# The first MoE's weight transfers on GpSimd's queue instead of SyncE's, in an attention + two-MoE kernel

## The chip, the cores and the metric

The kernel runs on one core of a Trainium2 chip. The metric is the device time of one execution in microseconds, lower being better. Before the change it is 1120.15 us, the median of three runs from 1114.83 to 1122.45.

## The reference

Three stages follow each other. All inputs are float32 in the reference; the weights reach the device as 64-bit floats.

```
# attention: batch 4, 12 heads, 448 tokens, head width 64
q_n, k_n = rmsnorm(q, g_q), rmsnorm(k, g_k)
attn = softmax(q_n @ k_n^T / sqrt(64));  attn_out = attn @ v
x = attn_out as [1792 tokens, 768]
# first MoE (one expert, no routing): 768 -> 1024 -> 768
h = x @ w_in;  solu = h * softmax(h);  ln = layernorm(solu) * g_ln;  x = ln @ w_out
# second MoE: 768 -> 2048 -> 768
h = x @ w_in;  g = h - tanh(h);  out = g @ w_out
```

## The kernel before

Products that need more than TensorE's reduced float32 are made of three matmuls: every operand is split into a high and a low part (`split`, the two halves of `w`), and `three` (L181 to L184) adds high x high, high x low and low x high. So a weight tile has two halves, each as large as the float32 weights.

**Weights.** `Stream` (L96 to L178) hands out a list of weight tiles in the order of their use. A tile is a 256 x 512 or 512 x 256 piece of a matrix in the form that the device gets (pairs of 32-bit words), 512 KB. `fetch` loads it raw (L115) into one of two buffers `raw`; `convert` turns the 64-bit values into float32 on ScalarE and VectorE, makes the high part on ScalarE and the low part on GpSimd (L161, for the input matrices) or VectorE (L155, for `w_out` of the first MoE). The result, again 512 KB, lies in one of five buffers `w`. With `save` it is stored to device memory (L164), and where the list names a tile a second time (`again`), L174 reloads that stored form instead. The first MoE's stream is `ws`: 12 tiles of `w_in` and 12 of `w_out` are loaded raw, converted and stored, `w_in` is reloaded for three of the four token blocks and `w_out` for all four. The second MoE's stream, `w2`, loads and converts 48 tiles and stores none.

**Order of the work.** Attention goes by pairs of heads, 24 in all. Its steps stand in a list sorted by slots, two slots a pair: keys and queries are loaded, normalised (`norm`, its last step `qn` at L258 on GpSimd), transposed and split (`qk_trans`), and copied by SyncE's transfers to other partitions (L301, L305 for queries, L307, L308 for keys). `maxima` gives the row maxima, `spread` puts them into the query tile by a small transfer (L355), `weights` makes the exponentials, `pv` the product with the values, `x_norm` divides and stores the result to `xd` (L432). `load_v` clears a value tile on GpSimd (L222) and loads it (L224, L228).

The first MoE goes over four token blocks `b` (384, 384, 384 and 640 tokens). `stage(b)` reads a block of attention's output (`x_split`, L496), makes the block's input product (`moe_h`, matmuls into `hps`, four quarters of 256 columns, three weight tiles each), its layer norm (one power on GpSimd at L563 for each 128 tokens), and the output product of the block before (`moe_x2`, into `x2ps`). `moe_h` asks for the next quarter's three tiles after the first tokens of the current one, by

```
if t0 == blocks[b][0][0] and tp == 0:
    ws.conv(w0 + 3 * qq + 6)
```

`overlap` writes the steps of a batch's attention between those of a stage in proportion to estimated costs. The second MoE follows, apart from its first six tiles and its first inputs, which are converted ahead of the first MoE's last stages.

The engines don't run in the written order exactly: the launch makes `TileContext(nc, schedule_with_timeline_sim=True)`, whose scheduler simulates times and lets each engine take the next instruction that is ready by its account. The order on each engine is then fixed, and each engine runs it strictly in turn. Waits on buffers are put in by the same layer. All transfers are issued by SyncE but three tiny ones of constants, which ScalarE issues.

Of the kernel before, what the change touches and what calls it, by code (L numbers as in the profile page):

```python
# [8 lines left out]
F32 = mybir.dt.float32  # L9
# [9 lines left out]
def kernel(  # L19
# [14 lines left out]
    nc = tc.nc  # L34
# [47 lines left out]
    def source(kind, i):  # L82
        if kind == "out":
            d, half = divmod(i, 2)
            src = moe_w_out[512 * half:512 * half + 512, 256 * d:256 * d + 256]
            return src.rearrange("(c p) (f z) -> p c f z", p=128, z=2), (4, 128)
        r, c = divmod(i, 3)
        if kind == "out2":
            src = moe2_w_out[256 * r:256 * r + 256, 512 * c:512 * c + 512]
        else:  # L90
            src = (moe_w_in if kind == "in" else moe2_w_in)[256 * c:256 * c + 256, 512 * r:512 * r + 512]
        return src.rearrange("(c p) (f z) -> p c f z", p=128, z=2), (2, 256)

    saved = {}

    class Stream:  # L96


        def __init__(self, items, pool, save):
            self.items, self.pool, self.save = items, pool, save  # L100
            self.raw, self.got = {}, {}
            self.nl = self.nc = 0
# [8 lines left out]
        def fetch(self, kind, i):  # L111
            if (kind, i) not in self.raw:
                src, (a, b) = source(kind, i)
                t = self.raw[kind, i] = raw_p.tile([128, a, b, 2], I32, tag="raw", name="raw64")
                nc.sync.dma_start(out=t, in_=src)  # L115

        def convert(self, kind, i, pool, save):
            self.fetch(kind, i)
            t = self.raw.pop((kind, i))
            a, b = t.shape[1:3]  # L120
            if kind == "out2":

                if i % 3 == 0:
                    self.wide = pool.tile([128, 2, a, 3 * b], F32R, tag="w18", name="w18")
                w = self.wide[:, :, :, b * (i % 3):b * (i % 3) + b]
            else:
                w = pool.tile([128, 2, a, b], F32R, tag="w6", name="w6")
            val = raw_p.tile([128, a, b], I32, tag="val", name="val")
            hi32 = t[:, :, :, 1].rearrange("p c f -> p (c f)")
            lo32 = t[:, :, :, 0].rearrange("p c f -> p (c f)")  # L130
            vv = val.rearrange("p c f -> p (c f)")

            fv, fh = vv.bitcast(F32), hi32.bitcast(F32)
            if save:
                nc.scalar.activation(out=fv, in_=fh, func=AF.Abs)
                nc.vector.tensor_scalar(out=fv, in0=fv, scalar1=2.0 ** -15, scalar2=None, op0=ALU.max)
            else:
                nc.gpsimd.tensor_scalar(out=fv, in0=fh, scalar1=2.0 ** -15, scalar2=None, op0=ALU.max)
                nc.vector.scalar_tensor_tensor(out=fv, in0=fh, scalar=-1.0, in1=fv, op0=ALU.mult, op1=ALU.max)
            nc.vector.tensor_scalar(  # L140
                out=vv, in0=vv, scalar1=3, scalar2=0x3FFFFFFF,
                op0=ALU.logical_shift_left, op1=ALU.bitwise_and,
            )
            nc.vector.scalar_tensor_tensor(
                out=vv, in0=hi32, scalar=-0x40000000, in1=vv, op0=ALU.bitwise_and, op1=ALU.bitwise_or
            )
            nc.vector.scalar_tensor_tensor(
                out=vv, in0=lo32, scalar=29, in1=vv, op0=ALU.logical_shift_right, op1=ALU.bitwise_or
            )
            x = val.bitcast(F32)  # L150
            if kind == "out":
                for c in range(4):
                    g = gln[:, 4 * (i % 2) + c:4 * (i % 2) + c + 1]
                    nc.scalar.activation(out=w[:, 0, c], in_=x[:, c], func=AF.Copy, scale=g)
                    nc.vector.scalar_tensor_tensor(  # L155
                        out=w[:, 1, c], in0=x[:, c], scalar=g, in1=w[:, 0, c].bitcast(F32),
                        op0=ALU.mult, op1=ALU.subtract,
                    )
            else:
                nc.scalar.activation(out=w[:, 0], in_=x, func=AF.Copy)  # L160
                nc.gpsimd.tensor_tensor(out=w[:, 1], in0=x, in1=w[:, 0].bitcast(F32), op=ALU.subtract)  # L161
            if save:
                saved[kind, i] = dram.tile([128, 2, a, b], F32, name=f"w_{kind}_{i}")
                nc.sync.dma_start(out=saved[kind, i], in_=w.bitcast(F32))  # L164
            return w

        def conv(self, n):
            while self.nc < min(n, len(self.items)):
                self.load(self.nc + 1)
                kind, i, again = self.items[self.nc]  # L170
                if again:
                    a, b = source(kind, i)[1]
                    w = self.pool(kind, i).tile([128, 2, a, b], F32R, tag="w6", name="w6")
                    nc.sync.dma_start(out=w.bitcast(F32), in_=saved[kind, i])  # L174
                else:
                    w = self.convert(kind, i, self.pool(kind, i), self.save)
                self.got[self.nc] = self.wide if kind == "out2" else w
                self.nc += 1  # L178
                self.load(self.nc + 2)
# [307 lines left out]
    Bp = {}  # L487
# [162 lines left out]
    items, w_at = [], {}  # L650
    for b in range(NBK + 1):
        for d in range(KD + 1):
# [3 lines left out]
            if d < KD and b > 0:  # L656
                w_at["out", b - 1, d] = len(items)
                items += [("out", i, True) for i in (2 * d, 2 * d + 1)]
    ws = Stream(items, lambda kind, i: Bp["w"], True)


    attn_next()
# [61 lines left out]
    items = []  # L724
    for sp in range(NSP):
        items += [("in2", 3 * sp + i, False) for i in range(3)]
        items += [("out2", 3 * sp + i, False) for i in range(3)]
    w2 = Stream(items, next_w, False)
    xs_t, ob = [], {}

    def x2_load(i):
# [109 lines left out]
```

## Time and profile before

| | before |
|---|---|
| median of three runs | 1120.15 us (1114.83 to 1122.45) |
| the profiled execution's own time | 1117.29 us |
| its span in the profile | 1115.4 us |
| TensorE busy (PE) | 1045.5 us, 94% |
| VectorE (DVE), ScalarE (ACT), GpSimd (POOL) busy | 694.8, 493.8, 234.2 us |
| moved by DMA | 171.20 MB, 153 GB/s over the span |
| chain that ended last, by engine | PE 74%, DMA 12%, DVE 7%, ACT 5% |

PE is TensorE's matmuls and PEld its weight loads; DVE is VectorE, ACT ScalarE, POOL GpSimd, SP or SPq SyncE's queue. L12 is line 12 of the kernel. In names such as `w<-w_in` the tile that is written stands in front of what is read; `w_in<-w` is a store of converted weights, `raw<-in_moe_w_in_dram` a raw load, and digits are dropped, so that the second MoE's raw loads bear the same names. A "wait" is idle time of an engine, with what ended it. The chain of waits is followed back from the last instruction, at each step to what released it. The clock column is the granted share of TensorE's full clock.

### The profile page before, as it was taken

To read this page: it belongs to the slowest core of one execution; us is meant where nothing else is said; L and a number is where in the kernel's file an instruction comes from. 1 tells how busy PE (TensorE), PEld (TensorE's weight loads), DVE (VectorE), ACT (ScalarE), POOL (GpSimd) and SP (SyncE) were. 2 spreads that over 40 slices of the span, in tenths; PEclk is the share of its full clock that TensorE was granted. 3 is DMA by queue.
4 is the path that set the end of the run, shared out by engine and by line. 5 is a ranking of instruction groups with operands and counts; after the bars stand their busy time and mean duration, and the time that the engine had idled before them with its cause. 6 is when DMAs were issued, how large, how long until landed. Compare 5 with 4: busy or idle time off the path is not lost.

```text
span 1115.4 us, 15528 instructions
## 1 busy us (share of the span) xinstructions
PE 1045.5 (94%) x5528; PEld 874.9 (78%) x5528; DVE 694.8 (62%) x1313; ACT 493.8 (44%) x1004; POOL 234.2 (21%) x204
## 2 busy tenths in 40 slices
PE   4989999988987899998999999999999999999998
PEld 2555666657774778777899989898999989898987
DVE  8776687788797353724655057375767666675444
ACT  4677777777676454744246154321212121212110
POOL 2411123131102000001500025242314241322000
PEclk9999999999998999998999999999999999999999
DMA  7987779957997978655767443121111111120004
GB/s 184 258 230 192 184 213 282 229 167 209 288 285 231 307 207 260 182 174 174 249 205 242 156 152 92 34 65 49 57 38 57 58 58 57 57 57 1 1 29 170
DMA packets 108945, 171.20 MB, mean 153 GB/s; under 512 B 31748, under 2 KB 73156, under 8 KB 108868
## 3 DMA queue, kind: packets, MB, share of 16 engines
q1 hardware_dynamic: 107568, 170.20, 52.2%
q8 instruction: 44, 0.72, 0.3%
q14 instruction: 33, 0.27, 0.1%
q10 hardware_dynamic: 1300, 0.01, 0.1%
HBM read 109.32 MB, written 29.10 MB: 124 GB/s over the span
## 4 chain that ended last, share of the span: by engine, by line
PE 74%; DMA 12%; DVE 7%; ACT 5%; issue 2%; SPq 1%; POOL 0%; ACTq 0%; DVEq 0%; POOLq 0%
PE pvps L401 8%; PE ops L183 7%; PE ops L184 7%; PE ops L182 7%; PE h2ps L183 7%; PE h2ps L184 7%; PE h2ps L182 7%; PE sps L378 4%; PE x2ps L182 3%; PE x2ps L183 3%; PE x2ps L184 3%; PE hps L182 2%; PE hps L184 2%; DMA xr<-xd 2%; PE hps L183 2%; DMA q<-wq 2%
## 5 line engine op out<-in xcount | busy, mean ns | idle before, releaser
L780 DVE TENSOR_TENSOR ob<-ops,ob 128x384 f32<-128x384 f32 x196 | 108.6, 555 | 103.0 <-PE ops L184 102.4
L161 POOL TENSOR_TENSOR w<-val,w 128x512 fp32r<-128x512 f32 x60 | 81.3, 1356 | 419.7 <-ACT w L160 402.6
L401 PE MATMUL pvps<-pf,va 128*128 128x448 f32 (+1 forms) x384 | 160.9, 583 | 1.7 <-ACT pf L387 1.7
L183 PE MATMUL ops<-w,gT 128*128 128x384 f32 x448 | 150.7, 336 | 0.0
L182 PE MATMUL ops<-w,gT 128*128 128x384 f32 x448 | 150.6, 336 | 0.0
L184 PE MATMUL ops<-w,gT 128*128 128x384 f32 x448 | 150.5, 336 | 0.0
L343 DVE TENSOR_REDUCE nm<-mps 128x1 f32<-128x448 f32 x168 | 102.9, 620 | 66.3 <-PE mps L342 57.6
L183 PE MATMUL h2ps<-x2s,w 128*128 128x512 f32 (+1 forms) x384 | 141.0, 367 | 0.0
L184 PE MATMUL h2ps<-x2s,w 128*128 128x512 f32 (+1 forms) x384 | 140.9, 367 | 0.0
L182 PE MATMUL h2ps<-x2s,w 128*128 128x512 f32 (+1 forms) x384 | 140.6, 367 | 0.0
L378 PE MATMUL sps<-q,k 128*128 128x448 f32 (+1 forms) x368 | 117.5, 413 | 20.7 <-ACT pf L387 9.2
L757 ACT ACTIVATE th<-h2ps 128x512 f32<-128x512 f32 (+1 forms) x64 | 34.8, 544 | 181.2 <-PE h2ps L184 180.9
L378 PEld LDWEIGHTS sps<-q,k 128*128 128x128 f32 (+1 forms) x368 | 63.0, 186 | 55.5 <-ACT pf L387 17.8
L387 ACT ACTIVATE pf<-sps 128x448 f32<-128x448 f32 x167 | 88.3, 539 | 37.9 <-PE sps L378 29.5
L182 PE MATMUL hps<-w,xs 128*128 128x256 f32 x336 | 101.0, 301 | 2.7 <-DMA w<-w_in 2.5
L184 PE MATMUL hps<-w,xs 128*128 128x256 f32 x336 | 96.5, 288 | 0.0
L183 PE MATMUL hps<-w,xs 128*128 128x256 f32 x336 | 95.6, 285 | 0.0
L401 PEld LDWEIGHTS pvps<-pf,va 128*128 128x128 f32 (+1 forms) x384 | 61.6, 195 | 42.1 <-issue 34.3
L342 PE MATMUL mps<-k,q 128*128 128x448 f32 (+1 forms) x144 | 77.2, 545 | 14.9 <-DVE nm L343 5.6
L258 POOL TENSOR_TENSOR qn<-qk,rr 112x512 f32<-112x512 f32 x44 | 47.5, 1101 | 192.5 <-DVE rr L239 88.9
L183 PEld LDWEIGHTS ops<-w,gT 128*128 128x128 f32 x448 | 84.3, 188 | 4.6
L182 PEld LDWEIGHTS ops<-w,gT 128*128 128x128 f32 x448 | 84.2, 188 | 4.6 <-DVE ob L780 0.2
(117 smaller groups left out, 2091.7 us busy)
## 6 DMA issues: line engine op xcount, KB each, us to landing
w<-w_out SPq DMA_DIRECT2D x48, 512.0 KB
raw<-in_moe_w_in_dram SPq DMA_DIRECT2D x36, 512.0 KB
raw<-in_moe_w_out_dram SPq DMA_DIRECT2D x36, 512.0 KB
w<-w_in SPq DMA_DIRECT2D x36, 512.0 KB
k<-wk SPq DMA_DIRECT2D x46, 224.0 KB
q<-wq SPq DMA_DIRECT2D x46, 224.0 KB
w_in<-w SPq DMA_DIRECT2D x12, 512.0 KB
w_out<-w SPq DMA_DIRECT2D x12, 512.0 KB
```

Of the source, the lines that this page charges most:

```text
L161: nc.gpsimd.tensor_tensor(out=w[:, 1], in0=x, in1=w[:, 0].bitcast(F32), op=ALU.subtract)
L182: nc.tensor.matmul(ps, lhsT=a[0], rhs=w[0], start=first, stop=False)
L183: nc.tensor.matmul(ps, lhsT=a[0], rhs=w[1], start=False, stop=False)
L184: nc.tensor.matmul(ps, lhsT=a[1], rhs=w[0], start=False, stop=last)
L258: eng.tensor_tensor(out=qn[:, a].rearrange("p c h d -> p h c d"), in0=t[:, a], in1=rr[:, a].rearrange("p h (c o) -> p h c o", o=1).to_broa ...
L342: nc.tensor.matmul(ps, lhsT=qh[:, f:f + 128], rhs=kh, start=True, stop=True)
L343: nc.vector.tensor_reduce(out=nm_t[p][:, c:c + 1], in_=ps, axis=AX.X, op=ALU.max, negate=True)
L378: nc.tensor.matmul(o, lhsT=K[p % NQ][:, i, z, k0:k0 + m], rhs=qcols(Q[p % NQ], slice(0, 128), p, i, z), start=(z == 0), stop=(z == 1))
L387: nc.scalar.activation(out=x, in_=ps, func=AF.Exp)
L401: nc.tensor.matmul(pv_t[n], lhsT=w, rhs=pc_t.pop((n, j))[r], start=first, stop=last)
L757: nc.scalar.activation(out=th, in_=ps, func=AF.Tanh)
L780: nc.vector.tensor_tensor(out=o, in0=ps, in1=o, op=ALU.add)
```

## The change

The stream gets the issuing engine as an argument. `ws`, the first MoE's stream, gets GpSimd, and `w2`, the second's, SyncE as before. So 24 raw loads, 24 stores and 84 reloads, 132 transfers of 512 KB, are issued by GpSimd.

```
-        def __init__(self, items, pool, save):
+        def __init__(self, items, pool, save, queue):
+            self.queue = queue
...
-                nc.sync.dma_start(out=t, in_=src)
+                self.queue.dma_start(out=t, in_=src)
...
-                nc.sync.dma_start(out=saved[kind, i], in_=w.bitcast(F32))
+                self.queue.dma_start(out=saved[kind, i], in_=w.bitcast(F32))
...
-                    nc.sync.dma_start(out=w.bitcast(F32), in_=saved[kind, i])
+                    self.queue.dma_start(out=w.bitcast(F32), in_=saved[kind, i])
...
-    ws = Stream(items, lambda kind, i: Bp["w"], True)
+    ws = Stream(items, lambda kind, i: Bp["w"], True, nc.gpsimd)
...
-    w2 = Stream(items, next_w, False)
+    w2 = Stream(items, next_w, False, nc.sync)
```

## Rows read from the trace of the kernel before

**Rows 1.** Busy time by stretch: stretch us, engines' busy us (instructions), clock, DMA share, GB/s

```profile
0.00:60.00 60.00, 42.40 (x124) 23.71 (x124) 46.41 (x107) 34.09 (x73) 21.19 (x29) 1.00 0.87 227
...
180.00:240.00 60.00, 54.66 (x278) 38.94 (x279) 46.61 (x96) 43.73 (x92) 12.38 (x12) 0.97 0.89 229
...
300.00:360.00 60.00, 48.46 (x207) 33.19 (x208) 52.66 (x125) 43.56 (x97) 9.12 (x11) 0.91 0.86 260
...
540.00:600.00 60.00, 58.95 (x444) 57.65 (x443) 38.55 (x93) 27.00 (x52) 13.66 (x12) 1.00 0.70 233
600.00:700.00 100.00, 99.51 (x591) 93.47 (x590) 42.78 (x56) 38.69 (x69) 22.48 (x14) 1.00 0.44 141
700.00:1060.00 360.00, 360.00 (x1910) 329.97 (x1909) 228.95 (x391) 77.02 (x136) 98.11 (x66) 1.00 0.15 45
...
0.00:600.00 600.00, 534.97 (x2768) 404.79 (x2768) 399.36 (x826) 371.26 (x789) 113.58 (x124) 0.98 0.79 226
```

**Rows 2.** Waits of TensorE over the span: total us, times, longest us

```profile
PE qkps L268 <- DVE nr L238: 11.0, 1, 11.0
...
PE sps L378 <- DMA q<-nt: 6.3, 4, 2.0
...
PE mps L342 <- DMA q<-wq: 3.4, 2, 1.8
...
PE hps L182 <- DMA w<-w_in: 2.5, 2, 2.0
...
PE x2ps L182 <- DMA w<-w_out: 1.7, 3, 0.6
```

**Rows 3.** The chain of waits in order of time, transfers: start us, us, what

```profile
13.77 6.93 DMA raw<-in_moe_w_in_dram
...
24.21 5.15 DMA q<-wq
...
202.76 8.00 DMA w<-w_in
...
285.76 7.97 DMA q<-wq
...
386.18 9.26 DMA xr<-xd
...
525.93 2.80 DMA xr<-xd
...
542.30 4.79 DMA w<-w_in
```

**Rows 4.** Waits of SyncE's queue, 0 to 600 us: total us, times, longest us

```profile
SPq L115 <- DVE val L147: 32.4, 13, 8.5
SPq L174 <- PE x2ps L184: 30.0, 16, 4.6
SPq L174 <- PE hps L184: 26.9, 16, 9.8
```

**Rows 5.** SyncE's issues by line: duration ns min/median/max, first and last start us

```profile
L174 SPq DMA_DIRECT2D w<-w_out x48: 319/320/1065, 316.3 to 629.6; - x48
L174 SPq DMA_DIRECT2D w<-w_in x36: 320/384/1610, 202.2 to 565.3; - x36
...
L115 SPq DMA_DIRECT2D raw<-in_moe_w_out_dram x17: 373/387/3250, 179.7 to 560.6; - x17
```

**Rows 6.** GpSimd's instructions by line: busy us, mean ns, idle before, releasers

```profile
L258 POOL TENSOR_TENSOR qn<-qk,rr 112x512 f32<-112x512 f32 x44 | 47.5, 1101 | 192.5 <-DVE rr L239 88.9 <-ACT w L154 20.7 <-PE hps L184 19.2
```

**Rows 7.** Timelines of GpSimd, SyncE and TensorE around 542 us: start us, us

```profile
540.07 1.99 POOL L138 TENSOR_SCALAR val<-raw 128x512 f32<-128x512 f32 x1 [1.98 <-DMA raw<-in_moe_w_out_dram]
...
542.30 1.67 SPq L174 DMA_DIRECT2D w<-w_in  x3
...
547.14 0.39 PE L182 MATMUL hps<-w,xs 128*128 128x256 f32 x1 [0.41 <-DMA w<-w_in]
```

## The prediction

> **What bounds the kernel now.** The table by stretch comes first [rows 1]. From 600 us on, in the second MoE, TensorE is busy for 99.51 of 100 us and then 360.00 of 360, and of the moved transfers only the last reloads fall there; nothing is to be won behind that point. Ahead of it lie attention and the first MoE, in which all of the moved transfers run. There TensorE is busy 42.40 of the first 60 us and 54.66, 48.46 and 58.95 in the three other 60-us stretches shown; over the 600 us it is idle for 65 us, of which 17.6 lie in the first 60. The same rows show the DMA engines 0.70 to 0.89 busy: this half is close to DMA-bound as well as close to TensorE-bound.
>
> What TensorE waits for by name is little [rows 2]: 11.0 us once at the start for VectorE, 6.3 + 3.4 us for the small transfers of attention's queries, and 2.5 + 1.7 us for the first MoE's weights. But engines run in order, and a late transfer holds up ScalarE or SyncE before it shows on TensorE. So the chain of waits says more [rows 3]. Between 0 and 600 us, pieces of the chain that are transfers which stay on SyncE's queue (keys and queries, their shifted copies, maxima, attention's output) number 14, the constants' load apart, from the one at 24.21 to the one at 525.93, and sum to 70.6 us. The moved kind (raw weights, stores, reloads) has 8 pieces, from 13.77 to 542.30, sum 48.5 us. A piece is 2.80 us where the queue is quiet and 7.97 or 9.26 us where weights are ahead of it: that difference is what the change can get at.
>
> **What the change does, part by part.** All 132 transfers of 512 KB (24 raw loads, 24 stores, 84 reloads) leave SyncE for GpSimd; sizes, order in the program, buffers and waits stay. Nothing is computed more or less.
>
> *SyncE is relieved.* A moved issue has cost it 0.32 to 0.39 us at the median, and up to 3.25 us when the queue was backed up [rows 5]. By the medians, with the 24 stores put at a raw load's, that is 84 x 0.35 + 48 x 0.39 = 48 us of issuing. It also stood at the head of its queue for 32.4 us until a raw buffer, and 30.0 + 26.9 us until a weight buffer came free [rows 4]; in that time nothing of attention that was queued behind could be issued (a few of the 13 stops on raw buffers are the second MoE's, which stay). None of this is lost one for one, as SyncE is no computing engine: it counts where a staying transfer is late, which is the 70.6 us above. If each of the 14 pieces fell to some 3 us, as the quietest of them, the chain would lose 70.6 - 42 = 28.6 us. That is the far end. The near end is 0: half the bytes in this stage are still the weights', and the engines that move them are the same. I take a third, -9.5 us, because the busy share of the DMA engines stays and because when a transfer comes earlier the next-latest (ScalarE's or VectorE's work, which has the shares of busy time in [rows 1]) takes over.
>
> *The start.* The raw load at 13.77 holds ScalarE's in-order queue for 6.93 us, and the query's copy after it takes another 5.15 [rows 3]. On a queue of its own the raw load can be issued before SyncE is through with the first keys, queries and values. That may take off up to 6.9 us, or cost up to 5.2 when 512 KB loads share the engines with the first heads' inputs. I take -2.
>
> *GpSimd takes 132 issues.* The trace has no transfer issued by GpSimd, so its price is bounded: below by nothing, since GpSimd is busy for only 114 of the 600 us [rows 1] and may do it in idle time; nearest by one of its own ordinary instructions, 1.10 us [rows 6]; above by the longest issue that SyncE had, 3.25 us [rows 5]. I take 1.1 us: 132 x 1.1 = 145 us, spread over 600 us with those 114 in them. It fits. What else is queued on GpSimd behind an issue that waits: the normalised keys and queries (44 of the instructions in [rows 6]) and the clearing of the value tiles. The first stand a whole slot ahead of their transposition in the written order (slot s - 3 against s - 2 and s - 1, two slots a head pair), which covers some microseconds; the clearing waits for TensorE just as the reloads do, in the same order. I put 0 on both; if that cover is gone, a wait of GpSimd for VectorE's norms, 88.9 us in all [rows 6], is what a reload would sit behind. The 14 powers of the layer norm have no such cover: VectorE goes on with their result. One issue in front of every one would be 14 x 1.1 = 15 us of VectorE, off the bound; I put 0 on it, and up to 5 in the range.
>
> *The tight reloads.* In the first MoE's input product, a quarter of the columns needs three weight tiles, five buffers exist, so the third tile of the next quarter is asked for only when TensorE lets go of the first of the current one. By the code that is 3 times in each of 3 blocks: nine reloads. [Rows 7] show one: issued at 542.30, TensorE has 0.41 us of idle time and starts on it at 547.14; the chain has the transfer as 4.79 us [rows 3]. So the lead, about 4.8 us, is spent to the end. An issue of 1.1 us in place of 0.38 adds 0.7 us to each: 9 x 0.7 = +6 us, the value I take; it is 0 if the clear ring gives it back, and the upper end is 9 x (1.1 + 2.0) = 28 us if GpSimd has an instruction of its own as long as the 1.99 us one in [rows 7] in front of each. In the last block that is likely for some, since GpSimd then converts the second MoE's first weights; I add 1.5 us.
>
> The Trainium skill has a price for the same step: "DMA: Bandwidth & Descriptors", section Latency and other measured facts, puts the first byte of a transfer from GpSimd at about 1 us and from SyncE at about 0.6; by it alone the tight reloads would cost 9 x 0.4 = 3.6 us in place of 6 (an estimate from that page), and no row here shows GpSimd's queue.
>
> **Sum.** -9.5 - 2 + 6 + 1.5 = -4 us. The profiled execution took 1117.29 us, of which the span is 1115.4; so 1117.3 - 4 = 1113 us. It lies 3 us under the median of the three runs shown (1120.15), whose own spread is 7.6 us. About 1% is what a measurement of this kernel can tell from no change, and the forecast is 0.6% under the median.
>
> **Rivals.**
> *A, the ring was the brake.* Small transfers no longer stand behind 512 KB ones: the full 28.6 us and the start's 6.9 come off, 1117.3 - 35.5 = 1082 us. For it: pieces of 7.97 and 9.26 us against 2.80 [rows 3]. Against it: TensorE is idle for only 65 us before 600 [rows 1], and just 9.7 of them are put to the queries' transfers [rows 2].
> *B, the reloads arrive late.* Issuing on GpSimd costs a tight reload more than its lead allows: +28 us, no gain elsewhere, 1117.3 + 28 = 1145 us. Its place is the nine third tiles; it decides from the point where a reload takes over 4.8 us from release to landing, and each further microsecond is 9 us. For it: the 0.41 us wait at 547.14 shows no reserve, and in the last block TensorE has no attention left to put in between. Against it: today only 4.2 us of TensorE's waits are put to these weights [rows 2], and a moved reload stops competing for its issue with attention's.
> *C, nothing.* The transfers share the same engines, and TensorE's stream stays the limit: 1117 us, and 1120 against the median. For it: the DMA share of 0.79 over the 600 us [rows 1] doesn't change with the queue. The Trainium skill says so outright: in "DMA: Bandwidth & Descriptors", section Issuing engines are not separate DMA queues, transfers of all issuing engines interleave on the same 16 DMA engines, and a second issuer saves only issue time. Here the issue time is the 48 us above on an engine that is not the bound.
>
> One thing has no price in the trace: the instruction order on every engine comes from a scheduler that simulates times (the launch says so), so the moved issues also rearrange other work. That may be a few microseconds either way and is part of the width.
>
> **How the numbers follow.** Forecast (a small gain, around 1113) 0.40; A 0.20; B 0.20; C 0.20. Faster by over 1% (below 1109) is A and a third of the forecast: 0.20 + 0.14 = 0.34. Slower by over 1% (over 1131) is most of B and a little of the rest, 0.20. The rest is 0.46. The range reaches half way into A and into B: 1088 to 1141, which leaves about one in ten out on either side.
>
> **What the profile after would show.** SyncE with 132 issues fewer, and 132 of them on GpSimd, each at 1 to 1.5 us; a longer one speaks for B. In the chain, the 14 staying pieces: a mean of 5.0 us now, 4.3 by my sum, about 3 by A, 5 by C. TensorE's wait for the first MoE's input weights: 2.5 us now, some 9 by my sum, 30 by B. The stretches behind 700 us must be unchanged. The prediction goes wrong if an issue on GpSimd costs several microseconds, if GpSimd's own waits stand in front of reloads for long (then normalised keys and queries come late as well), or if the rearranged order moves the start by more than it has been given here.

## The result and the profile after

The changed kernel takes 1134.28 us (median of four runs, 1131.98 to 1136.04) against 1121.3 us for the kernel before on the same chip: ratio 1.0132, interval 1.0101 to 1.0163, slower. The profiled execution took 1133.72 us, span 1131.9. The time lies inside the range, but on the other side of no change from the forecast of 1113.

Busy time by stretch, columns as in [rows 1] (stretch, engines' busy us and instructions, clock, DMA share, GB/s):

```profile
0.00:60.00 60.00, 37.36 (x92) 20.96 (x93) 45.25 (x98) 26.90 (x59) 27.87 (x39) 1.00 0.79 218
...
360.00:420.00 60.00, 50.36 (x254) 39.45 (x253) 27.34 (x53) 29.98 (x61) 15.91 (x23) 0.91 0.86 260
540.00:600.00 60.00, 57.06 (x445) 56.85 (x444) 35.93 (x66) 18.17 (x41) 23.48 (x27) 0.97 0.64 223
...
700.00:1060.00 360.00, 360.00 (x1921) 330.60 (x1920) 233.25 (x395) 83.29 (x150) 104.01 (x70) 1.00 0.17 49
0.00:600.00 600.00, 528.30 (x2688) 396.76 (x2689) 399.58 (x789) 360.25 (x772) 180.77 (x240) 0.97 0.76 219
```

TensorE (first column) does 37.36 us of work in the first 60 us where it did 42.40, and 528.30 against 534.97 in the first 600. GpSimd (fifth) rises from 113.58 to 180.77, which is the issues: 120 of the 132 moved transfers fall into this stretch and take 71.3 us. From 700 to 1060 us TensorE is busy throughout, as before.

TensorE's waits (total us, times, longest), for [rows 2]:

```profile
PE qkps L269 <- DVE qn L259: 16.7, 3, 12.6
...
PE sps L379 <- DMA q<-nt: 5.1, 2, 3.4
...
PE mps L343 <- DMA q<-nt: 3.1, 1, 3.1
...
PE hps L183 <- DMA w<-w_in: 2.4, 2, 1.7
...
PE x2ps L183 <- DMA w<-w_out: 1.7, 3, 1.0
```

The wait for the first MoE's weights hasn't moved (2.4 and 1.7 us, before 2.5 and 1.7): no reload is late. The start is (16.7 against 11.0). The chain's transfers of the middle (start us, us), for [rows 3]:

```profile
206.79 7.75 DMA q<-wq
...
373.99 8.58 DMA k<-wk
...
382.59 13.21 DMA q<-wq
...
395.82 4.57 DMA k<-wk
...
402.33 3.03 DMA q<-wq
...
425.12 6.91 DMA w<-w_in
```

Between 0 and 600 us the chain now has 17 pieces that are transfers which stayed on SyncE, from 29.50 to 538.45 us, sum 83.6 us, mean 4.9; before it was 14, 70.6 and 5.0. The moved kind has 4 pieces, 34.4 us, in place of 8 with 48.5. GpSimd's issues, 0 to 600 us (busy us, mean ns, idle before), for [rows 5, 6]:

```profile
L175 POOL DMA_DIRECT2D w<-w_in x36 | 19.8, 551 | 90.0 <-PE hps L185 61.6 <-PE x2ps L185 25.6 <-PE mps L343 1.9
L175 POOL DMA_DIRECT2D w<-w_out x36 | 19.3, 537 | 65.5 <-PE x2ps L185 41.2 <-PE hps L185 16.2 <-PE mps L343 3.7
...
L116 POOL DMA_DIRECT2D raw<-in_moe_w_out_dram x12 | 9.4, 786 | 30.7 <-ACT e L549 14.1 <-ACT w L155 7.7 <-DVE nm L344 3.2
```

An issue costs GpSimd 0.54 to 0.79 us on average, by kind of transfer: half to three quarters of the 1.1 us taken.

Where the time is lost is read best from the same piece of work in each kernel. The table has its start before and how much later it starts in each run below: the 8th group of four key or query transpositions (end of the fourth head pair), the first value product of pairs 4, 12, 16, 18, 19, 21 and 24, and the last output product of the first MoE, of one profiled execution each.

```
                       qk8  pv4   pv12  pv16  pv18  pv19  pv21  pv24  x2 last
before, at us         58.0  82.9 209.6 297.8 342.4 384.7 431.2 494.3  644.7
changed               +9.5  +5.2  +7.6  +6.7  +5.8  +9.2 +11.2 +12.8  +16.8
e1_in_raw_sync        -2.8  -0.1  -0.9  +0.3  -0.8  +6.8  +4.2  +5.9   +6.1
e3_reload_only        -4.4  -2.7  -1.6  -3.4  +1.6  -0.5  -0.5  +1.4   +0.7
e4_first_two          +7.7  +6.0  +7.4  +9.8  +9.9 +10.5 +11.1 +11.6  +10.7
e6_first_two_late     +5.5  +5.7  +6.4  +5.9  +4.1  +5.5  +6.1  +7.6  +11.5
e7_in_reload_only     +3.2  +2.1  +1.7  +3.2  +7.9 +17.3 +14.7 +16.8  +18.5
e8_in_raw_out_reload  -2.5  -0.7  +2.1  +2.1  -1.1  +4.8  +8.4 +10.1  +14.7
p_before_order_after +10.9 +11.0 +12.0 +12.8 +16.9 +18.2 +19.5 +21.0  +21.5
p_after_order_before  +4.5  +4.5  +8.9 +11.7 +12.0 +19.1 +22.5 +27.1  +31.6
p_first_two           +3.9  +5.2  +4.8  +4.1  +2.6  +2.4  +2.6  +2.7   +2.3
p_after_less_two      +6.5  +9.2 +11.4 +13.3 +10.2 +17.7 +24.2 +29.0  +34.7
p_reload_only         -3.7  -1.2  +5.4  +8.0  +5.6 +10.9 +12.8 +16.4  +19.2
p_load_store          +2.4  +4.0  +6.4  +7.3 +11.0 +12.9 +12.6 +14.4  +14.8
p_in_reload           -3.1  -0.4  -0.7  +0.7  -0.8  +4.2  +9.5 +10.1  +15.4
p_in_reload_held      -1.0  -1.1  -0.9  +6.0  +6.0  +5.4  +9.2 +15.6  +22.2
p_after_held          +2.9  +6.4 +10.5 +24.6 +23.1 +28.2 +30.6 +33.3  +40.2
```

In these traces the change loses 5 us or more at the start, 5 more around 360 to 430 us, and the rest towards the first MoE's end; all of it ahead of 662 us.

The table has to be read with care, as single executions differ by themselves. p_reload_only, p_in_reload and p_in_reload_held are the kernel before, order included, up to their first moved transfer (at 206.7, 200.5 and 201.6 us), and yet they stand at -3.7, -3.1 and -1.0 in the first column and at +5.4, -0.7 and -0.9 in the third. So 5 us in one cell show nothing alone. The trace of e7 is also 8 us slower than the median of its runs, that of p_after_order_before 5, that of p_reload_only 4, and e3's is 4 us faster.

### The profile page after: what moved, and what is told of

The parts are those of the page before. It is cut to its first block, busy times and chain, and to the rows that moved or that the text cites. A ratio compares the mean times of both kernels' runs of the same rounds, so it can differ in the third digit from the quotient of the medians.

```text
span 1131.9 us, 15574 instructions
## 1 busy us (share of the span) xinstructions
PE 1053.5 (93%) x5528; PEld 881.4 (78%) x5528; DVE 706.3 (62%) x1313; ACT 495.2 (44%) x1004; POOL 310.5 (27%) x336
## 4 chain that ended last, share of the span: by engine, by line
PE 69%; DMA 11%; DVE 9%; issue 5%; ACT 4%; POOL 1%; SPq 0%; DVEq 0%; ACTq 0%; POOLq 0%
PE ops L184 7%; PE h2ps L184 7%; PE h2ps L185 7%; PE h2ps L183 7%; PE ops L185 7%; PE ops L183 7%; PE pvps L402 7%; PE sps L379 3%; DMA xr<-xd 2%; PE x2ps L183 2%; PE hps L183 2%; PE x2ps L185 2%; PE x2ps L184 2%; PE hps L184 2%; PE hps L185 2%
## 5 line engine op out<-in xcount | busy, mean ns | idle before, releaser
L379 PE MATMUL sps<-q,k 128*128 128x448 f32 (+1 forms) x368 | 119.3, 419 | 14.8 <-ACT pf L388 7.0
L184 PEld LDWEIGHTS ops<-w,gT 128*128 128x128 f32 x448 | 84.2, 188 | 4.7
L183 PEld LDWEIGHTS ops<-w,gT 128*128 128x128 f32 x448 | 84.1, 188 | 4.4
L185 PEld LDWEIGHTS ops<-w,gT 128*128 128x128 f32 x448 | 84.1, 188 | 0.0
```

The costliest lines, as they stand in the source:

```text
L183: nc.tensor.matmul(ps, lhsT=a[0], rhs=w[0], start=first, stop=False)
L184: nc.tensor.matmul(ps, lhsT=a[0], rhs=w[1], start=False, stop=False)
L185: nc.tensor.matmul(ps, lhsT=a[1], rhs=w[0], start=False, stop=last)
L379: nc.tensor.matmul(o, lhsT=K[p % NQ][:, i, z, k0:k0 + m], rhs=qcols(Q[p % NQ], slice(0, 128), p, i, z), start=(z == 0), stop=(z == 1))
```

## The experiments

Three theories stood at first. S: GpSimd issues two raw loads at 3.0 us, and 1 MB then stands beside the first heads' inputs. M: a second queue takes a share of the 16 DMA engines away from attention's small transfers. O: the scheduler's rearranged order costs the time, whatever the queue.

**Parts of the change, order left to the scheduler.** In the cuts below, which are shortened, e4 is the kernel before with only the first two raw loads on GpSimd; e6 is the changed kernel with these two waiting for a constant (they go out at 9.0 us); e1 has w_in's raw loads back on SyncE; e3 has only the reloads on GpSimd.

```
e4  (self.queue if kind == "in" and i < 2 else nc.sync).dma_start(out=t, in_=src)    # only this
e6  if kind == "in" and i < 2:
        nc.gpsimd.tensor_copy(out=t[:, 0, 0, 0:1].bitcast(F32), in_=gam)
e1  (nc.sync if kind == "in" else self.queue).dma_start(out=t, in_=src)
e3  nc.sync.dma_start for L116 and L165; self.queue for L175
```

> The kernel before, with the first two raw loads alone issued by GpSimd. S expects the start's delay and nothing else: 5 to 6 us, 1.0045 to 1.0055, a third key pair transposed near 35 us. M expects 1.000. O expects 1.000 plus or minus 0.5%, with no fixed place for it.

> The changed kernel, but its first two raw loads wait for the constants gam (one extra one-column copy on GpSimd into each of the two raw tiles, which the load overwrites), so that GpSimd issues them at about 9 us instead of 3; all 132 transfers stay on GpSimd. S expects 4 to 6 us less than the changed kernel, 1.008 to 1.010, although the queue is the same. M expects 1.013, no difference. If the start stays late although the loads come at 9 us, S is wrong about the time of issue.

> The changed kernel, but the 12 raw loads of the first MoE's w_in are back on SyncE; w_out's raw loads, all stores and all reloads stay on GpSimd. Theory S (start): of the 16.5 us by which the span grew, 5 to 6 come from two raw loads that GpSimd issues at 3 us, which share the DMA engines with the first heads' keys, queries and values. S expects the start back at the old times (first keys of the third pair transposed near 30 us, not 35) and a ratio of about 1.008 to 1.010 to the kernel before. Rival M (sharing): the loss lies in the reloads that share the engines with attention's small transfers all along; it expects 1.013 as before. Rival O (order): the loss comes from the rearranged instruction order alone; it expects any ratio between 0.99 and 1.015, and the start may stay late.

> Only the 84 reloads are on GpSimd; raw loads and stores are on SyncE as before. S expects no late start and, if the start is all, 1.000 to 1.003. M expects most of the loss, 1.008 to 1.012, with long query and key copies between 360 and 420 us. The prediction's own terms (SyncE relieved, no rival for the first inputs, reloads issued at once) expect 0.985 to 0.995. O: anything within 1%.

Measured: e4 1126.98 us (ratio 1.0076, 1.0047 to 1.0105), e6 1128.54 (1.0105, 1.0076 to 1.0134), e1 1126.34 (1.0076, 1.0049 to 1.0104), e3 1121.25 (1.0030, 1.0006 to 1.0054), before 1117.86. (The ratios and intervals are estimated from all runs of both kernels, so that a ratio needn't be the quotient of the two medians.) In e4 two loads alone make the start 6 to 8 us late, and cost more than S had named (1.0045 to 1.0055). In e6 it stays 5.5 us late although the loads go out at 9.0 us, which by the expectation speaks against the time of issue as S's reason. With w_in's raw loads on SyncE (e1, e3) the start isn't late, and 3 to 6.5 us are lost between 298 and 385 us. That looked like S and M together, each with its place.

**Is the middle w_out's reloads?** e7 leaves only w_in's 36 reloads on GpSimd, e8 is e1 with w_out's 48 reloads back on SyncE as well.

```
(nc.sync if kind == "out" else self.queue).dma_start(out=w.bitcast(F32), in_=saved[kind, i])
```

> Only the 36 reloads of w_in are issued by GpSimd; raw loads, stores and the 48 reloads of w_out stay on SyncE. Beside the run with all 84 reloads on GpSimd (1121.25, ratio 1.003) the one difference is w_out's reloads. M (w_out's reloads, issued in bursts from a second queue, crowd out attention's small transfers between 335 and 410 us): the 3 to 4 us that that run was ahead until 330 us are kept, the waits of TensorE for q<-nt between 335 and 410 us (5.9 us there) go back under 2, and the time is 3 to 4 us under before's, ratio 0.997. O (only the rearranged order counts): no such link, the ratio stays within 1.000 to 1.006 and the loss may lie anywhere.

> The changed kernel with w_in's raw loads and w_out's reloads back on SyncE: GpSimd issues w_out's raw loads, all stores and w_in's reloads. Beside the run with only w_in's raw loads back (1126.34, ratio 1.0076) the one difference is w_out's reloads. S and M together (start and w_out stage are the two places of the loss): both are gone, 1115 to 1119 us, ratio 0.997 to 1.001, and the delay that the other run took between 360 and 390 us (+7) is under 2. O: ratio stays near 1.0076. If stores or w_out's raw loads on GpSimd cost something of their own, 1122 or more with the delay elsewhere.

Measured: e7 1129.05 us (1.0102, 1.0058 to 1.0147), e8 1130.02 (1.0081, 1.0050 to 1.0112), before 1120.29. Both expectations of M fell: with fewer transfers moved than in e3, e7 is slower, and its trace loses 9 us between 342 and 385 us. e8 is as slow as 1122 or more, which was named for a cost of stores or w_out's raw loads, but with its delay at the same place as e1's. w_out's reloads aren't the cause, and the sizes of parts don't add up. That spoke for O, though e7 lies above O's range too (1.000 to 1.006).

**Order and queue apart, a first try.** Both kernels with the simulated schedule switched off.

> The kernel before, with the scheduler's simulation of times switched off, so that the engines run nearly in the written order. It is the partner of the next run, not a test by itself: slower than before by some per cent is expected by every theory, as the written order is not tuned for the engines' queues.

> The changed kernel, with the scheduler's simulation of times switched off. Beside the run before it (same setting) all engines but SyncE and GpSimd have the same order, so that no rearrangement of computing can make a difference. O: the two are equal within 4 us. S (early raw loads on their own queue crowd out the first heads' inputs): the partner's start is late by 5 us or more and the kernel is slower than its partner by 5 to 20 us. If SyncE in the written order was held up much more by the weights than in the tuned order, the queue change may instead gain, and that would say that the relief of SyncE is real but the tuned order had used it up already.

Measured: 1233.77 us (n_before) and 1212.69 (n_after): here the change gains 21 us. The premise didn't hold, though: the two orders differ as well (in the two traces, 904 of the 5528 places in TensorE's order of matmuls and 559 of ScalarE's 1004 hold another operation), so the pair doesn't tell order from queue. It does show that the sign belongs to the schedule and not to the queue as such.

**Order and queue apart.** The program has the same instructions in both kernels. So the order in which the scheduler put one kernel was written down and forced on the other, on all five engines, by edges that only order the issue (shortened):

```
for n in order_of_the_other_kernel:
    i = traced[n]
    if i.engine in last:
        tc.add_manual_dep(i, last[i.engine], DependencyInfo(DependencyClass.NoSync, ...))
    last[i.engine] = n
```

> The changed kernel (all 132 transfers issued by GpSimd) with every engine held to the instruction order of the kernel before; a moved transfer takes the place in GpSimd's order that the scheduler gave it among GpSimd's instructions before. O (the rearranged order is the loss): 1120 or less, ratio 1.000 or under, and the gain that the pair without the simulated schedule showed (21 us) may show in part. Queue theories (S, crowding by the second queue): as slow as the changed kernel, 1130 to 1137, ratio 1.010 to 1.015, with the third and fourth head pairs 5 us late or more.

> The counterpart: the kernel before (all transfers on SyncE), with every engine held to the order that the scheduler gave the changed kernel. O: as slow as the changed kernel or slower, 1130 or more, ratio 1.010 or more. Queue theories: 1115 to 1124, ratio within 0.996 to 1.003. If both this and its counterpart are slower than before, each order fits only its own queue, and the loss of the change is then the queue in a new order that mends a part of it.

> The changed kernel in the order of the kernel before, with only the first two raw loads left on SyncE (130 transfers on GpSimd). S (the two early loads take the engines from the first heads' inputs): 8 to 9 us faster than the same without this exception, and the third and fourth head pairs on time within 2 us. If S was a matter of the rearranged order, within 3 us of it.

> The kernel before in its own order, with only the first two raw loads on GpSimd. The same edit with a free order cost 0.8% (1126.98 against 1117.86). S: again 1124 to 1129, ratio 1.005 to 1.010, third and fourth head pairs 5 us late or more. O: 1116 to 1122, ratio within 0.997 to 1.003.

| | order of the kernel before | order of the changed kernel |
|---|---|---|
| weights on SyncE | 1117.53 | 1137.05, ratio 1.0163 (1.0140 to 1.0187) |
| weights on GpSimd | 1143.37, ratio 1.0228 (1.0201 to 1.0254) | 1134.28 (beside 1121.3), ratio 1.0132 (1.0101 to 1.0163) |

Neither O nor a queue theory says this table, but the third possibility that was written down does: each order fits its own queue. The queue alone costs 26 us, the order alone 20, and the new order gives back some 10 of the queue's 26. p_first_two is 1121.77 us (1.0033, 1.0013 to 1.0053), less than half of what e4 lost; it also bounds what the forced order costs by itself, as no run holds a kernel to its own order with nothing else changed. p_after_less_two is 1151.80 (1.0299, 1.0269 to 1.0329), slower than with the two loads on GpSimd. So S falls as the account of the whole loss: more than half of e4's 9 us was its order.

**Which transfers, in the old order.**

> All engines in the order of the kernel before, only the 84 reloads on GpSimd. The whole change in this order costs 26 us, of it 21 behind 160 us, where the reloads lie from 200 us on. M: the reloads are most of that, ratio 1.009 to 1.018 (10 to 20 us), with the loss behind 240 us. If GpSimd's loads and stores are what costs, ratio under 1.005.

> All engines in the order of the kernel before, only the 24 raw loads and 24 stores on GpSimd. M with both parts adding up: ratio 1.005 to 1.014, 4 to 6 us of it in the first 60 us. If the reloads are not the greater part, ratio 1.015 or more.

> All engines in the order of the kernel before, only the 36 reloads of w_in on GpSimd. The same edit with a free order cost 1.0% (1129.05 against 1120.29), 8 us of it between 330 and 370 us, though w_out's reloads stayed on SyncE. If that was the rearranged order: ratio within 0.998 to 1.004 here. If it was the queue: 1.008 or more again, with the jump in the same stretch.

Measured against 1118.61: reloads alone 1133.38 us (1.0121, 1.0085 to 1.0157), raw loads and stores alone 1130.85 (1.0102, 1.0070 to 1.0133), w_in's 36 reloads alone 1133.03 (1.0122, 1.0079 to 1.0165). With the order held, the parts add up within their intervals, which reach some 4 us to either side of each: 14.8 + 12.2 = 27 against 26 us. The whole of the reloads' 14.8 us is w_in's, 14.4. So the queue is enough for a loss like e7's, and e3 had the luckier order.

**What TensorE's clock adds.** The granted clock has two levels in these traces, 1.00 (2.4 GHz) and 0.50 (1.2 GHz). In p_after_order_before TensorE works for 0.13 of the 4.90 us up to 360.9 us, and then the clock is at the lower level for 10.2 us (columns as in [rows 1]):

```profile
356.00:360.90 4.90, 0.13 (x1) 0.00 (x0) 0.92 (x2) 1.77 (x3) 0.00 (x0) 1.00 0.80 214
360.90:371.10 10.20, 7.96 (x15) 4.30 (x15) 10.16 (x26) 8.75 (x17) 6.87 (x9) 0.50 0.41 138
```

Every run has its mean clock on record, and (1 - clock) x span is the most that the lower level can have cost it. As a mean of all runs that is 32.0 us for the whole change in the old order, against 20.6 for the kernel before beside it; 26.2 for the reloads alone, 28.0 for raw loads and stores and 24.9 for w_in's reloads, against 19.0. So up to 11 of the 26 us, and up to 9 of the 12 of raw loads and stores, aren't late data but TensorE at half its clock. In the new order it adds nothing: 20.4 us on SyncE's queue, 21.0 on GpSimd's.

**Do two queues share?** Transfers alone, with SyncE's transfer (2 KB, 224 KB or 384 KB) and four 512 KB reloads in different positions, four times each (the cases in short); the time runs from SyncE's issue to the ScalarE instruction that reads the result.

```
def sync_ahead(kind): issue_bulk(nc.sync, 4); critical(kind)      # critical: always SyncE
def pool_ahead(kind): issue_bulk(nc.gpsimd, 4); critical(kind)    # issued some 1.6 us behind the first, 0.1 to 0.2 us ahead of the fourth
def pool_same(kind):  issue_bulk(nc.gpsimd, 4) and critical(kind) at the same time
def sync_behind(kind): critical(kind); issue_bulk(nc.sync, 4)
```

> Not the reference's computation: transfers alone, each of three kinds of staying transfer (2 KB of maxima, 224 KB of keys, 384 KB of attention's output) issued by SyncE alone, with four 512 KB reloads behind it on SyncE, with four on GpSimd at the same time, with one on GpSimd, with four ahead of it on SyncE, and with four ahead of it on GpSimd. M (two queues share the engines, one queue serves in order): with four behind it on its own queue the transfer takes what it takes alone, within 0.5 us; with four on GpSimd at the same time it takes at least 1 us longer for the 224 and 384 KB kinds, and with four ahead on GpSimd less than with four ahead on SyncE. Against M: no difference between behind on SyncE and at the same time on GpSimd, within 0.3 us; then the slower small transfers of the kernel come from something else.

```
us, lowest to highest of 4    2 KB           224 KB         384 KB
alone                         1.76 to 3.11   2.81 to 2.87   2.88 to 3.08    (3.11: the first of all)
four behind it, SyncE         1.71 to 1.76   2.90 to 2.97   2.90 to 3.12
four at the same time, GpSimd 1.70 to 1.74   2.94 to 3.09   2.92 to 3.04
one at the same time, GpSimd  1.69 to 1.72   2.87 to 2.94   2.92 to 3.10
four ahead of it, SyncE       5.35 to 6.45   8.26 to 8.53   6.44 to 7.62
3 ahead, 1 beside, GpSimd     4.93 to 6.07   7.74 to 7.94   6.79 to 7.66
```

One case of each of the last two rows in the timeline (start us, us, what); the length of SyncE's own row holds its wait for the next case, and the ScalarE row is the arrival:

```profile
304.26 0.37 SPq L69 DMA_DIRECT2D bulk_d<-saved_d  x1
...
304.80 13.02 SPq L56 DMA_DIRECT2D kk<-wk  x2
...
313.30 0.20 ACT L113 ACTIVATE f_k_sync_ahead<-kk 64x1 f32<-64x1 f32 x1 [14.75 <-DMA kk<-wk]
...
316.43 0.53 POOL L69 DMA_DIRECT2D bulk_b<-saved_b  x1
...
316.95 0.53 POOL L69 DMA_DIRECT2D bulk_c<-saved_c  x1
...
317.47 0.53 POOL L69 DMA_DIRECT2D bulk_d<-saved_d  x1
...
325.09 0.20 ACT L113 ACTIVATE f_k_pool_ahead<-kk 64x1 f32<-64x1 f32 x1 [11.58 <-DMA kk<-wk]
```

M's expectation falls here: a transfer that is issued first isn't slowed by what comes behind it, on either queue (0.3 us at most). But one that is issued behind 512 KB transfers waits for them whichever queue they are on: 8.26 to 8.53 us behind four of SyncE's, 7.74 to 7.94 behind three of GpSimd's and beside a fourth. In the second case shown SyncE issues the copy at 317.34 us (the end of its row less the issue's 0.47 us), and from 317.4 to 321.4 us only GpSimd's queue, q0, moves anything (packets, MB, share of the 16 engines):

```profile
q0 software_dynamic: 357, 1.33, 93.3%
```

What counts for these transfers is the moment of issue. But they are short bursts, and in the changed kernel, where both queues have work for longer, M's sharing does show. Queues from 386 to 393 us, q1 being SyncE's:

```profile
q0 software_dynamic: 402, 1.45, 72.1%
q1 hardware_dynamic: 403, 0.63, 33.3%
```

The queues move as many packets, but GpSimd's are 3.6 KB on average and SyncE's 1.6 KB, so that the reloads get more than twice the bytes. A reload that GpSimd issued at 385.63 us takes 10.0 us and lands no later than the query's copy that SyncE had issued 3 us ahead of it (382.59, 13.21 us). In the kernel before SyncE's queue had the engines to itself while the same pair's queries were copied, here from 378 to 385 us:

```profile
q1 hardware_dynamic: 787, 1.35, 90.3%
```

**Does the moment of issue explain the kernel?** A new theory, J (jump-ahead): SyncE's strict order kept a reload that had its buffer early behind attention's transfers that stood in front of it; on GpSimd it goes out when the buffer is free and stands ahead of them. In both held runs every moved transfer also waits until the last transfer that SyncE had issued 3 us or more ahead of it in the kernel before has landed.

```
tc.add_manual_dep(moved, that_transfer, DependencyInfo(DependencyClass.Sync, ...))
```

> The kernel before in its own order with w_in's 36 reloads on GpSimd, as in the run that gave 1133.03 (ratio 1.0122), but each reload now also waits until the last transfer that SyncE had issued 3 us or more ahead of it in the kernel before has landed. Nothing else differs. Jump-ahead (a second queue doesn't share or favour, the engines serve in order of issue, and the loss is that a reload goes out the moment its buffer is free, ahead of attention's transfers that SyncE's strict order had kept in front): the jump between 370 and 400 us (from -1 to +6, then +10 by 440) is gone, the time is 1116 to 1124, ratio 0.998 to 1.005. If the loss comes from GpSimd issuing at all: 1.010 or more again.

> The whole change in the order of the kernel before (1143.37, ratio 1.0228), with the same hold for all 132 moved transfers. Jump-ahead: at least half of the 26 us comes back, ratio 1.000 to 1.011; what remains is the hold's own lateness (a landing is 2 to 3 us later than an issue) and GpSimd's instructions that now stand behind a held transfer. If GpSimd's issuing, or the packets of its queue, are the cause: 1.018 or more.

Measured against 1118.94: 1139.64 us (1.0159, 1.0107 to 1.0211) and 1155.61 (1.0323, 1.0267 to 1.0380). In total both are a miss: the hold makes it slower, not faster. In the stretch for which the jump was named the traces look as J says, though. Three w_in reloads around 380 us, p_in_reload (GpSimd's first, then SyncE's queries):

```profile
374.73 0.62 POOL L175 DMA_DIRECT2D w<-w_in  x1
...
377.79 0.53 POOL L175 DMA_DIRECT2D w<-w_in  x1 [2.43 <-PE x2ps L185]
...
380.30 0.53 POOL L175 DMA_DIRECT2D w<-w_in  x1 [1.98 <-PE x2ps L185]
...
377.08 0.64 SPq L302 DMA_DIRECT2D q<-wq  x1
...
378.67 0.47 SPq L306 DMA_DIRECT2D q<-wq  x1
```

The same in the kernel before:

```profile
377.78 0.63 SPq L301 DMA_DIRECT2D q<-wq  x1
...
385.27 0.85 SPq L174 DMA_DIRECT2D w<-w_in  x2
...
388.61 0.61 SPq L174 DMA_DIRECT2D w<-w_in  x1
```

And in p_in_reload_held:

```profile
382.52 0.64 SPq L302 DMA_DIRECT2D q<-wq  x1
...
385.31 0.61 SPq L306 DMA_DIRECT2D q<-wq  x1
...
390.23 1.15 POOL L175 DMA_DIRECT2D w<-w_in  x2 [9.20 <-DMA x2d<-x]
...
392.91 0.53 POOL L175 DMA_DIRECT2D w<-w_in  x1 [1.52 <-PE pvps L402]
```

A copy of this pair's queries is a piece of the chain in all three, but not the same one of the four copies: the first before, the second in p_in_reload, the fourth in p_in_reload_held. From the issue of the first of the four (377.78, 377.08, 382.52) to the end of the piece it is 5.5 us before, 10.4 with the reloads in front and 6.4 with the reloads held back. The pieces, in the order before, p_in_reload, p_in_reload_held:

```profile
377.78 5.53 DMA q<-wq
```

```profile
378.67 8.80 DMA q<-wq
```

```profile
385.31 3.57 DMA q<-wq
```

Between 342 and 385 us p_in_reload loses 5.0 us (table, -0.8 to +4.2), and the held run 0.6 less than nothing (+6.0 to +5.4), after it had lost 6.9 between 209.6 and 297.8. That is one execution each, and no more than such executions differ by: a sign for J, not a proof. Nor does it tell J from M, since with the reloads held back there is nothing beside the copies to share with. What the hold costs is another wait, TensorE's for these same weights, p_in_reload and then p_in_reload_held (before: 2.5 us, 2 times, [rows 2]):

```profile
PE hps L183 <- DMA w<-w_in: 7.2, 4, 3.3
```

```profile
PE hps L183 <- DMA w<-w_in: 17.5, 6, 3.9
```

So on these traces w_in's reloads have a narrow window: earlier, and they stand in front of queries; later, and TensorE waits for them. Some of them are late already without the hold (7.2 us), so that p_in_reload's loss isn't J's alone.

## Why the prediction was wrong, step by step

*What bounds the kernel*: right. Behind 700 us TensorE stayed busy, the loss is in the half that is close to DMA-bound, and its DMA share is as high as before (0.86 between 360 and 420 us).

*SyncE is relieved, -9.5 us*: the step that failed. It took the 7.97 and 9.26 us pieces of [rows 3] for time behind weights in SyncE's queue, which another queue would take away. The transfers alone show that such time is spent behind what was issued earlier, on whichever queue, and the kernel's trace that the other queue's packets are served beside SyncE's. In the changed kernel the staying pieces have the mean that rival C gave (4.9, named at 5), and there are more of them: 83.6 us in the chain in place of 70.6, so +13.0 where -9.5 was forecast. With the order held, the issue of the staying ones did come earlier against TensorE's work, but by little: for the 2 KB maxima 0.1 us on average from 60 to 160 us, 0.3 from 160 to 300 and about 2 from 300 to 430. Against that stands that w_in's reloads went out 6.2 us earlier between 300 and 430. The landing of the 2 KB transfers (`q<-nt`) shows what came of it; they are the only ones in packets of 512 bytes, so the last of its four packets gives each one's time. Between 160 and 600 us it takes 2.98 us on average before, 3.54 in the changed kernel and 3.89 in p_after_order_before (3.29, 4.90 and 5.05 between 300 and 430 us). By the number of 512 KB weight transfers issued in the 6.5 us ahead of it or up to 0.5 us behind, over eight of the traces (the two kernels, both swapped orders, p_first_two, p_reload_only, p_load_store, p_in_reload; two transfers more have six):

```
weights ahead   0     1     2     3     4     5
transfers     161    81    72    50    13     5
mean us      1.68  3.16  3.03  4.41  7.01  6.59
```

That number is 1.33 on average before, between 160 and 600 us, and 1.77 and 1.73 in the two others. The middle of the changed kernel is the plainest case. GpSimd's reloads around the query's copies (timeline):

```profile
372.04 0.53 POOL L175 DMA_DIRECT2D w<-w_out  x1 [1.67 <-PE x2ps L185]
...
374.64 1.05 POOL L175 DMA_DIRECT2D w<-w_out  x2 [2.07 <-PE x2ps L185]
...
378.77 0.54 POOL L175 DMA_DIRECT2D w<-w_out  x1 [3.08 <-DVE rr L240]
...
381.32 0.58 POOL L175 DMA_DIRECT2D w<-w_in  x1
...
382.41 0.55 POOL L175 DMA_DIRECT2D w<-w_in  x1 [0.51 <-PE x2ps L185]
...
382.59 0.47 SPq L306 DMA_DIRECT2D q<-wq  x1
```

Six reloads, 3 MB, in 11 us, and the copy at 382.59 takes 13.21 us as a piece of the chain.

*The start, -2 us*: wrong sign; 5 to 9 us were lost in the trace, at or past the bound of +5.2. The bound's reason fits (512 KB loads in front of the first heads' inputs): the two loads are issued at 3.00 and the third pair's keys at 17.52 us, before at 12.89. It was taken for the less likely end. It isn't the whole reason: in the old order the keys go out at 13.09 with all transfers on GpSimd, and 4.5 us are lost all the same. How much belongs to which load is not settled: the two alone cost 4 us in the old order and 6 to 8 with a free one, but in the old order leaving just them on SyncE doesn't help. With w_in's raw loads on SyncE there is no loss at the start in e1, e3, e8, p_reload_only and p_in_reload; in e7, which has another order, there are 2 to 3 us.

*GpSimd takes 132 issues*: 0.54 to 0.79 us each instead of 1.1, 78 us in all instead of 145, and no cover was missed that the waits show.

*The tight reloads, +6 us, and +1.5*: nothing. TensorE's wait for these weights stayed at 2.4 us, not the 9 forecast, because GpSimd issues a reload that it has waited for within 0.3 us of the release. Rival B falls with it for this reason; its mechanism exists all the same, and p_in_reload (7.2 us) and the held run (17.5 us) pay for it.

*Rival A* falls outright. *Rival C* named the right mechanism (the same engines, whichever the queue), but took it that nothing changes then. The Trainium skill, "DMA: Bandwidth & Descriptors", section Issuing engines are not separate DMA queues, says that transfers of all issuing engines interleave on the same DMA engines; the trace agrees (402 and 403 packets from 386 to 393 us). It also says that a second issuer only saves issue time, and there the measurement decides: with the order held it costs 26 us.

*The scheduler, left without a price*: it had one as large as anything in the sum. Held on SyncE, the new order costs 20 us; for GpSimd's queue it is worth 10. "A few microseconds either way" was too small by a factor of several. That the time still came out inside the range is luck: 26 us of queue less 10 of order, with neither in the sum.

*TensorE's clock* is in no term either. In the changed kernel it didn't matter, in the old order it did (up to 11 of 26 us).

*The sum* itself: 1113 lies 7 us under the median of 1120.15 and not 3, as the text has it; its 0.6% is right.

What stays open: how much of the queue's 26 us is the earlier issue (J), how much the sharing by packets (M) and how much reloads that come late; what the raw loads and stores cost in the old order behind the start (p_load_store goes from +4.0 to +14.8 between 83 and 645 us) beyond the clock's part; and whether GpSimd's own work in front of reloads has a part. The whole change with every transfer held (p_after_held) mixes the hold's lateness with it and doesn't answer that. No version with the simulated schedule was faster than the kernel before; e3 and p_first_two, 0.3% slower, come nearest.

## What to carry to other kernels

Moving bulk transfers to another engine's queue gave the small ones no free lane here: ask which transfers will be issued earlier by it, what stands behind them at that moment, and whose packets are larger where both queues have work. An in-order issue queue that seems to be in the way may be what keeps prefetches from running ahead of urgent transfers. Where a scheduler re-sorts the program, judge the parts of a change in a fixed order: with a free one the part with 36 transfers was slower than that with 84, with a fixed one the parts added up. And before a few microseconds between two traces are explained, see how far two traces of the same program lie apart at that place: here it was 5 us.

## What had not been expected of the hardware

Two queues that feed the same 16 DMA engines behaved in two ways. In the transfers alone they were almost one line: a 224 KB copy of SyncE's behind three 512 KB reloads of GpSimd's and beside a fourth took 7.74 to 7.94 us, behind four of SyncE's 8.26 to 8.53, alone 2.8, and in the case shown none of its packets moved for 4 us. In the changed kernel, with work in both queues, they moved equally many packets (402 and 403 from 386 to 393 us), which gave the queue with the larger packets more than twice the bytes. The Trainium skill, "DMA: Bandwidth & Descriptors", section SWDGE vs HWDGE vs iDMA, says that each DMA engine goes round-robin between the queues that the two kinds of issue feed. The changed kernel's trace agrees with that; the transfers alone show none of it for those 4 us (357 packets of one queue and none of the other), and there the measurement decides. Why the two differ no run here shows.
